# Attention, two expert layers and a planned order: five edits to the attention stage and its planner

## The chip, the cores and the metric

The kernel runs on one core of a Trainium2 chip, in one launch. The metric is device time in microseconds. Five engines have queues of their own that are worked off in order: TensorE (PE in the profile; PEld is its weight load, which runs beside its products), VectorE (DVE), ScalarE (ACT), GpSimd (POOL) and SyncE (SP, which here only issues DMAs). An engine waits for another through semaphores; whatever stands behind a waiting instruction in its queue waits too.

## The reference

Shapes: q, k, v are (4, 8, 1152, 64); the result of attention is taken as 2304 tokens of 512 values.

```python
q_pool = q.reshape(B, H, S // 2, 2, D).mean(axis=3)
scores = np.matmul(q_pool, k.transpose(0, 1, 3, 2)) / np.sqrt(D)
attn = np.exp(scores - np.max(scores, axis=-1, keepdims=True))
attn = attn / (np.sum(attn, axis=-1, keepdims=True) + 1e-09)
x = np.matmul(attn, v)                 # then (tokens, 512)
h = x @ w_in                           # 512 -> 2048
x = (h * np.cos(h)) @ w_out            # 2048 -> 512
expert = np.argmax(x @ w_gate, axis=1) # 8 experts, 512 -> 1024 -> 512
out[mask_e] = gate_w * (np.maximum(x[mask_e] @ w1[e], 0) @ w2[e])
```

## The kernel before, in words

The work has three stages: attention (lines 157 to 373), the first layer pair with the cosine (`layer1`, `layer2`, lines 802 to 836), and the experts (lines 862 to 880). The change touches attention, its planner, and the first weights of the second stage.

**Attention.** Two heads form a pair (the 64 values of a head fill half of the 128 rows), so there are 16 pairs, i = 0 to 15. For a pair, `load` (192) fetches q and K, `loadv` (200) V, `qadd` (204) adds the two halves of q that are pooled, `kh`, `qh` and `qt` (210 to 222) make rounded copies of K and Q on ScalarE. The maxima over keys are taken first, from products of the rounded copies: 14 tiles (t, g), of which t is a block of 128 queries (t = 4 the last half block) and g a third of the 1152 keys. `mx` (224) computes a tile into PSUM, `red` (236) reduces it on VectorE. `mneg` (250) joins the thirds and negates, `pmr` (256) turns the column into rows by a transposition on TensorE, `mrow` (261) copies them out of PSUM, and `mset` (266) brings them by DMA into row 0 and row 64 of the tile MR. The first pair does that in two parts, t = 0 to 2 and t = 3 and 4. The score step `s` (275) is a product of K and Q for one of 9 key blocks j and one of two halves hq of the queries, to which a product of a row of ones with MR adds the negated maximum. `exp` (283) is the exponential on ScalarE into a tile E, `es` (287) sums the E tiles on GpSimd, `pv` (294) multiplies with V into the accumulator o, and `ob`, `sum_`, `ln`, `rcp`, `nr1`, `nr2`, `norm` (300 to 332) divide by the sum and store the result in xT. The products of `s` and `mx` use TensorE as two row halves of 64, those of `pv` and `sum_` as two column halves: the row form and the column form.

**Splits.** Beside this, 32 jobs (`cload` to `cst`, lines 336 to 368) read the weights w_in and w_out, split each into a high and a low part on ScalarE and VectorE, and store them to the DRAM tensor ws. Each uses a PSUM bank of a pool `m` with a single buffer, which `pmr` and `sum_` use as well.

**The order** inside attention is written out by a planner. `steps` (33) lists every step with a due time, an engine, a cost in microseconds, what it reads and writes, and its pool. Due times are in units of their own: a pair takes 6 units, the s steps are a third of a unit apart, `pv` follows its s by 1.1 units, and split job n is due at 0.05 + 3 n. `plan` (102) then simulates: for each engine it looks among the pending steps that are due at most AHEAD units after the first pending one, and takes the one with the least

```python
late = max(0, t - free[e])*WAIT + P[n][0] + SWITCH*(e == "PE" and P[n][4] != mode)
```

that is, wait in us times WAIT, plus due time, plus SWITCH units if TensorE would have to change its form. The kernel's queues get the resulting order (371 to 373).

**The second stage** loads the 16 split weight tiles of 1 MB from ws (line 805) at its first block of 256 tokens, into tiles that share their memory with attention's, so that each load waits until what lay there is no longer read. `split_x` (638) prepares the first block of xT. For each weight tile, `layer1` (802) computes h by 12 products and passes it through nine steps on ScalarE and VectorE to g; `layer2` (829) multiplies g by the second half of the tile into po.

Of the kernel before, what the change touches and what calls it, by code (L numbers as in the profile page):

```python
# [28 lines left out]
AHEAD = {"PE": 5.4, "DVE": 3.6, "ACT": 3.0, "POOL": 3.9, "SP": 8.0}  # L29
WAIT, SWITCH = 2.75, 0.5  # L30


def steps(NP, NJ, J):


    P = []
# [5 lines left out]
    for i in range(NP):  # L42
        b = 6*i
        first = i == 0
        p = -101 if first else b - 11.8
        at(p - 9, "load", (i, 0), "SP", 0.6, (), [("qr", i)], ("qr", 2, ("qr", i)))
        at(p - 9, "load", (i, 1), "SP", 0.6, (), [("k", i)], ("k", 4, ("k", i)))
        at(b - 7, "loadv", (i,), "SP", 0.6, (), [("v", i)], ("v", 3, ("v", i)))
        at(p, "qadd", (i,), "DVE" if first else "POOL", 1.1 if first else 1.41, [("qr", i)], [("q", i)], ("q", 3, ("q", i)))
        at(p, "kh", (i, 0), "ACT", 0.63, [("k", i)], [("kh", i, 0)], ("kh", 2, ("kh", i, 0)))  # L50
        at(p + 0.5, "qh", (i,), "ACT", 0.63, [("q", i)], [("qh", i)], ("qh", 2, ("qh", i)))
        at(p + 1, "kh", (i, 1), "ACT", 0.63, [("k", i), ("kh", i, 0)], [("kh", i, 1)])
        at(-40 if first else p + 2.5, "qt", (i,), "ACT", 0.42, [("q", i)], [("qt", i % 2)])
        parts = ((0, 3), (3, 5)) if first else ((0, 5),)
        for lo, hi in parts:
            p = (-20 if lo else -100) if first else b - 8.95
            for n, (t, g) in enumerate(tiles):
                if lo <= t < hi:
                    x = p + n*(0.1 if first else 5.8/14)
                    ks = [[("kh", i, 0)], [("kh", i, 0), ("kh", i, 1)], [("kh", i, 1)]][g]  # L60
                    if t == 4: ks = [("kh", i, 0), ("kh", i, 1), ("qt", i % 2)]
                    else: ks = ks + [("qh", i)]
                    key = ("x", i, t, g)
                    at(x, "mx", (i, t, g), ROWS, 0.35 if (t, g) == (4, 0) else 0.18, ks, [key], ("s", 2, key) if first and n % 3 else ("x", 1, key))
                    at(x, "red", (i, t, g), "DVE", 0.56 if (t, g) == (4, 2) else 0.96, [key], [("mx", i, lo)])
            x = p + 2 if first else p + 5.7
            at(x, "mneg", (i, lo, hi), "DVE", 0.17, [("mx", i, lo)], [("mneg", i, lo)])
            at(x + 0.1, "pmr", (i, lo, hi), ROWS, 0.2, [("mneg", i, lo)], [("pmr", i, lo)], ("m", 1, ("pmr", i, lo)))
            at(x + 0.2, "mrow", (i, lo, hi), "DVE", 0.27, [("pmr", i, lo)], [("mrow", i, lo)])
            at(x + 0.2, "mset", (i, lo, hi), "SP", 2.4, [("mrow", i, lo)], [("mr", i, lo)])  # L70
        for hq in range(2):
            for j in range(J):
                m = b + 3*hq + j/3
                mr = [("mr", i, lo) for lo, hi in parts if hq or not lo]
                key = (i, hq, j)
                at(m, "s", key, ROWS, 0.617, [("k", i), ("q", i)] + mr, [("s", *key)], ("s", 2, ("s", *key)))
# [25 lines left out]
def plan(P):  # L102
# [15 lines left out]
    for i in range(1 + max(p[3][0] for p in P)):  # L118
        if ("kh", i, 1) in users:
            users["kh", i, 0] |= users["kh", i, 1]  # L120
# [818 lines left out]
```

## Time and profile before

| what | value |
|---|---|
| runs | 1249.96, 1252.36, 1255.13 us; median 1252.36 |
| profiled execution | 1250.38 us, its span 1248.7 us |
| granted TensorE clock, mean | 0.994 |
| TensorE busy | 1208.4 us, 97% of the span |
| VectorE, ScalarE, GpSimd busy | 872.7, 762.1, 432.9 us |
| attention | about 0 to 484 us |

A row of a timeline has the start and the length in us, the engine, the line of the kernel, the operation, what it writes and reads, how many instructions were merged, and in brackets the idle time of that engine before it and what ended it. SPq is SyncE's queue: a row there is the issue of a DMA, not its transfer. Products in fp32 appear as two instructions each, so one s step is four of line 279 and two of line 281, one pv step four of line 298.

### The profile page before, as it was taken

What the parts mean: (1) busy time and instruction counts of PE and PEld (TensorE: products, weight loads), DVE (VectorE), ACT (ScalarE), POOL (GpSimd) and SP (SyncE); (2) the same over time, 40 slices, a digit from 0 to 9 for tenths busy, and PEclk for the clock granted to TensorE, in tenths of its full rate; (3) what the DMA queues carried; (4) which work ended last, traced back from release to release, by engine and by line L of the source; (5) the groups of instructions that cost most, each with busy time, mean ns of one, the idle gap of its engine ahead of it and who ended that gap; (6) DMA issues with size and microseconds to landing.
All of it is one profiled execution on the core that took longest, in us unless ns stands there. A gap on an engine that the chain in (4) does not pass through costs nothing. (4 is left out here: it accounts for less than half of the span.)

```text
span 1248.7 us, 22742 instructions
## 1 busy us (share of the span) xinstructions
PE 1208.4 (97%) x8415; PEld 956.9 (77%) x8415; DVE 872.7 (70%) x1895; ACT 762.1 (61%) x1533; POOL 432.9 (35%) x380
## 2 busy tenths in 40 slices
PE   5999999999999998999999999999998999999997
PEld 2566666666665655899999999999987998999896
DVE  5877777777776743667767767777676877777761
ACT  2566666666666654565565565565574877677751
POOL 3678887888887784000000000000003121112100
PEclk9999999999999998999999999999999999999999
DMA  3644444444443348200000000000046997778720
GB/s 129 221 149 147 156 128 138 146 126 126 136 149 100 96 149 331 124 19 1 18 13 6 18 1 18 18 1 18 18 152 234 400 334 259 269 270 287 261 72 6
DMA packets 70411, 163.75 MB, mean 131 GB/s; under 512 B 7643, under 2 KB 24153, under 8 KB 68252
## 3 DMA queue, kind: packets, MB, share of 16 engines
q1 hardware_dynamic: 66300, 150.92, 35.1%
q0 software_dynamic: 4000, 11.38, 2.5%
q8 instruction: 66, 1.08, 0.4%
q14 instruction: 45, 0.37, 0.1%
HBM read 135.65 MB, written 28.39 MB: 131 GB/s over the span
## 5 line engine op out<-in xcount | busy, mean ns | idle before, releaser
L292 POOL TENSOR_TENSOR es<-es,E 128x576 f32<-128x576 f32 x192 | 277.6, 1446 | 33.8 <-ACT E L285 23.6
L285 ACT ACTIVATE E<-s 128x576 f32<-128x576 f32 x288 | 182.3, 652 | 111.2 <-PE s L281 104.4
L242 DVE TENSOR_REDUCE MX<-pmx 128x2 f32<-128x768 f32 x192 | 182.9, 957 | 88.8 <-PE pmx L231 88.0
L813 PE MATMUL h<-xh,wf 128*128 128x256 f32 x1152 | 233.1, 287 | 3.5 <-DMA wf<-ws 3.5
L834 PE MATMUL po<-wf,g 128*128 128x512 f32 x864 | 224.3, 395 | 4.3 <-ACT g L825 3.6
L813 PEld LDWEIGHTS h<-xh,wf 128*128 128x128 f32 x1152 | 189.9, 193 | 8.6 <-issue 4.2
L279 PE MATMUL s<-Q,K 64*128 64x288 f32 x1152 | 193.7, 420 | 1.9 <-ACT E L285 1.9
L679 POOL DMA_INDIRECT xg<-x2d,idx x25 | 27.5, 1099 | 474.1 <-ACT ar L818 390.3
L834 PEld LDWEIGHTS po<-wf,g 128*128 128x128 f32 x864 | 152.7, 189 | 33.4 <-ACT g L825 7.1
L668 DVE TENSOR_TENSOR w<-raw,w 128x1024 fp32r<-128x1024 f32 x128 | 154.3, 1221 | 22.0 <-ACT w L667 16.7
L298 PE MATMUL o<-E,vt 128*64 128x288 f32 x1152 | 165.5, 415 | 0.2 <-ACT E L285 0.2
L813 PE MATMUL h<-xl,wf 128*128 128x256 f32 x576 | 164.1, 285 | 0.0
L281 PE MATMUL s<-MR,ON 64*128 64x288 f32 x576 | 148.5, 511 | 0.0
L667 ACT CAST w<-raw 128x1024 fp32r<-128x1024 f32 x128 | 132.4, 1053 | 18.9 <-DMA raw<-in_moe_w_dram 10.3
L748 PE MATMUL po<-w,hh 128*128 128x512 f32 x600 | 142.6, 392 | 0.0
L748 PEld LDWEIGHTS po<-w,hh 128*128 128x128 f32 x600 | 110.9, 188 | 22.8 <-ACT hh L737 0.3
L822 ACT ACTIVATE ar<-ar 128x256 f32<-128x256 f32 x144 | 60.1, 417 | 98.9 <-DVE ar L821 98.5
L298 PEld LDWEIGHTS o<-E,vt 128*64 128x64 f32 x1152 | 73.6, 136 | 59.1 <-issue 19.4
L279 PEld LDWEIGHTS s<-Q,K 64*128 64x128 f32 x1152 | 96.8, 188 | 28.2 <-issue 14.6
L813 PEld LDWEIGHTS h<-xl,wf 128*128 128x128 f32 x576 | 111.1, 193 | 4.0
L713 PE MATMUL ph<-xh,w 128*128 128x256 f32 x576 | 111.4, 288 | 1.6 <-ACT xh L640 1.3
L824 DVE SCALAR_TENSOR_TENSOR ar<-ar,h 128x256 f32<-128x256 f32 x144 | 60.3, 419 | 54.1 <-ACT ar L823 54.0
(189 smaller groups left out, 1852.0 us busy)
## 6 DMA issues: line engine op xcount, KB each, us to landing
raw<-in_moe_w_dram SPq DMA_DIRECT2D x128, 512.0 KB
wf<-ws SPq DMA_DIRECT2D x16, 1024.0 KB
qr<-in_q_dram SPq DMA_DIRECT2D x16, 576.0 KB
K<-in_k_dram SPq DMA_DIRECT2D x16, 576.0 KB
vt<-in_v_dram SPq DMA_DIRECT2D x16, 576.0 KB
cv_t<-in_moe_w_in_dram SPq DMA_DIRECT2D x16, 512.0 KB
ws<-cv_o SPq DMA_DIRECT2D x32, 256.0 KB
cv_t<-in_moe_w_out_dram SPq DMA_DIRECT2D x16, 512.0 KB
```

The source lines that it names most:

```text
L242: nc.vector.reduce_max(out.rearrange("p (w g) -> p w g", g=3)[:, 2*t:2*t+2, g], p[:, :, :KG], axis=AX.X)
L279: nc.tensor.matmul(p[:, h, :NQ], lhsT=T["k", i][R[h], j*128:(j+1)*128], rhs=T["q", i][R[h], qs], start=True, stop=False)
L281: nc.tensor.matmul(p[:, h, :NQ], lhsT=ON[R[h]], rhs=MR[i % 3][R[h], qs], start=False, stop=True)
L285: nc.scalar.activation(e, T.pop(("s", i, hq, j))[:, :, :NQ], AF.Exp, scale=1.0/16)
L292: nc.gpsimd.tensor_add(T["es", i, hq], T["e", i, hq, 0] if j == 1 else T["es", i, hq], T["e", i, hq, j])
L298: nc.tensor.matmul(T["o", i, hq][64*h:64*h+64], lhsT=T["v", i][:, h, j], rhs=T["e", i, hq, j][:, h], start=(j == 0), stop=(j == J-1))
L667: nc.scalar.copy(w[:, 0], t)
L668: nc.vector.tensor_sub(w[:, 1], t, w[:, 0])
L713: nc.tensor.matmul(ph, lhsT=wt[k][:, a, m*128:(m+1)*128], rhs=x[k//2][y][:, k % 2], start=(c == 0), stop=(c == 3*KC-1))
L748: nc.tensor.matmul(po, lhsT=hs[m][:, y, q*128:(q+1)*128], rhs=wt[4 + m//2][:, a, (m % 2)*512:(m % 2)*512+512], start=(c == 0), stop=(c == ...
L813: nc.tensor.matmul(h, lhsT=w[:, a, k*128:(k+1)*128], rhs=x[k//2][y][:, k % 2], start=(n == 0), stop=(n == 3*KC-1))
L834: nc.tensor.matmul(pos[c][t], lhsT=g[:, y, t*128:(t+1)*128], rhs=W1[f][:, b, 512:], start=(f == 0 and i == 0), stop=(f == FT-1 and i == 2))
```

## The change

- The planner counts a change of form as 0.2 us into the column form and 0.1 into the row form, instead of 0.12 each; WAIT goes from 2.75 to 5.72, SWITCH from 0.5 to 0.7, and AHEAD changes for three engines. There are 12 E buffers instead of 10, and some costs and due times are altered.
- The loads of the first two pairs and the first V are due ahead of everything. The first pair's q and K are loaded, added and rounded in two pieces of columns each (the first 384, then the rest).
- The first part of the first pair's maxima goes to MR without a DMA: six products, each of one column of the maxima with the identity, write the rows to rows 0 and 64 of a PSUM bank, and VectorE and ScalarE copy one row each. The second part (t = 3 and 4) is due at -4 instead of -20.
- Split job n is due at 10.21 + 2.95 n, and from n = 27 on at 89 + 1.2 (n - 27).
- Four of the 16 weight tiles of the second stage get memory of their own, and are loaded from ws during attention, 8 units after the store that completes them is due.

```diff
...
 FETCH = {"load": 3.0, "loadv": 2.0, "cload": 2.0}
-AHEAD = {"PE": 5.4, "DVE": 3.6, "ACT": 3.0, "POOL": 3.9, "SP": 8.0}
-WAIT, SWITCH = 2.75, 0.5
+AHEAD = {"PE": 4.5, "DVE": 4.12, "ACT": 3, "POOL": 2.17, "SP": 8.0}
+CHANGE = {COLS: 0.2, ROWS: 0.1}
+EARLY = 4
+BEHIND = 1.1
+SPREAD = 5.1
+WAIT, SWITCH = 5.72, 0.7
...
-        p = -101 if first else b - 11.8
-        at(p - 9, "load", (i, 0), "SP", 0.6, (), [("qr", i)], ("qr", 2, ("qr", i)))
-        at(p - 9, "load", (i, 1), "SP", 0.6, (), [("k", i)], ("k", 4, ("k", i)))
-        at(b - 7, "loadv", (i,), "SP", 0.6, (), [("v", i)], ("v", 3, ("v", i)))
-        at(p, "qadd", (i,), "DVE" if first else "POOL", 1.1 if first else 1.41, [("qr", i)], [("q", i)], ("q", 3, ("q", i)))
-        at(p, "kh", (i, 0), "ACT", 0.63, [("k", i)], [("kh", i, 0)], ("kh", 2, ("kh", i, 0)))
-        at(p + 0.5, "qh", (i,), "ACT", 0.63, [("q", i)], [("qh", i)], ("qh", 2, ("qh", i)))
-        at(p + 1, "kh", (i, 1), "ACT", 0.63, [("k", i), ("kh", i, 0)], [("kh", i, 1)])
-        at(-40 if first else p + 2.5, "qt", (i,), "ACT", 0.42, [("q", i)], [("qt", i % 2)])
+        p = -101 if first else b - 12.5
+        early = -200 if i < 2 else b - 20.8
+        at(early, "load", (i, 0), "SP", 0.6, (), [("qr", i, 0)], ("qr", 2, ("qr", i, 0)))
+        at(early, "load", (i, 1), "SP", 0.6, (), [("k", i, 0)], ("k", 4, ("k", i, 0)))
+        if first:
+            at(early, "load", (i, 2), "SP", 0.6, [("k", i, 0)], [("k", i, 1)])
+            at(early, "load", (i, 3), "SP", 0.6, [("qr", i, 0)], [("qr", i, 1)])
+        at(-200 if first else b - 7, "loadv", (i,), "SP", 0.6, (), [("v", i)], ("v", 3, ("v", i)))
+        whole = range(1 + first)
+        for x in whole:
+            c = ((0.67, 0.33)[x] if first else 1)
+            at(p + 9*x, "qadd", (i, x), "DVE" if first and not x else "POOL", 1.45*c, [("qr", i, x)] + [("q", i, 0)]*x, [("q", i, x)], None if x else ("q", 3, ("q", i, 0)))
+            at(p + 0.1 + 9*x, "qh", (i, x), "ACT", 0.2 + 0.47*c, [("q", i, x)] + [("qh", i, 0)]*x, [("qh", i, x)], None if x else ("qh", 2, ("qh", i, 0)))
+        for x in range(2):
+            c = ((0.48, 0.76)[x] if first else 0.67)
+            at(p + (0.1 if first else 0.2 + 0.8*x), "kh", (i, x), "ACT", c, [("k", i, x*first)] + [("kh", i, 0)]*x, [("kh", i, x)], None if x else ("kh", 2, ("kh", i, 0)))
+        at(-4 if first else p + 2.5, "qt", (i,), "ACT", 0.48, [("q", i, whole[-1])], [("qt", i % 2)])
...
-            p = (-20 if lo else -100) if first else b - 8.95
+            p = (-4 if lo else -100) if first else b - 8.72
...
-                    x = p + n*(0.1 if first else 5.8/14)
+                    x = p + n*(0.1 if first else SPREAD/14)
...
-                    else: ks = ks + [("qh", i)]
+                    else: ks = ks + [("qh", i, x) for x in whole if t == 3 or not x]
...
-                    at(x, "mx", (i, t, g), ROWS, 0.35 if (t, g) == (4, 0) else 0.18, ks, [key], ("s", 2, key) if first and n % 3 else ("x", 1, key))
+                    at(x, "mx", (i, t, g), ROWS, 0.35 if (t, g) == (4, 0) else 0.19, ks, [key], ("s", 2, key) if p == -100 and n % 3 else ("x", 1, key))
...
-            x = p + 2 if first else p + 5.7
+            x = (-2 if lo else p + 2) if first else p + SPREAD
             at(x, "mneg", (i, lo, hi), "DVE", 0.17, [("mx", i, lo)], [("mneg", i, lo)])
+            if first and not lo:
+                at(x + 0.1, "pmq", (i,), ROWS, 1.2, [("mneg", i, lo)], [("pmr", i, lo)], ("m", 1, ("pmr", i, lo)))
+                for h in range(2):
+                    at(x + 0.2, "mput", (i, h), ("DVE", "ACT")[h], 0.45, [("pmr", i, lo)], [("mr", i, h - 2)])
+                continue
             at(x + 0.1, "pmr", (i, lo, hi), ROWS, 0.2, [("mneg", i, lo)], [("pmr", i, lo)], ("m", 1, ("pmr", i, lo)))
             at(x + 0.2, "mrow", (i, lo, hi), "DVE", 0.27, [("pmr", i, lo)], [("mrow", i, lo)])
             at(x + 0.2, "mset", (i, lo, hi), "SP", 2.4, [("mrow", i, lo)], [("mr", i, lo)])
...
                 m = b + 3*hq + j/3
-                mr = [("mr", i, lo) for lo, hi in parts if hq or not lo]
+                mr = [("mr", i, x) for x in ([-2, -1] + [3]*hq if first else [0])]
...
-                at(m, "s", key, ROWS, 0.617, [("k", i), ("q", i)] + mr, [("s", *key)], ("s", 2, ("s", *key)))
-                at(m, "exp", key, "ACT", 0.65, [("s", *key)], [("e", *key)], ("e", 10, ("e", *key)))
+                at(m, "s", key, ROWS, 0.617, [("k", i, x) for x in whole] + [("q", i, x) for x in whole if x < 1 or hq] + mr, [("s", *key)], ("s", 2, ("s", *key)))
+                at(m, "exp", key, "ACT", 0.65, [("s", *key)], [("e", *key)], ("e", 12, ("e", *key)))
...
-                    at(m, "es", key, "POOL", 1.41, [("e", *key)] + [("e", i, hq, 0)]*(j == 1), [("es", i, hq)], ("es", 2, ("es", i, hq)) if j == 1 else None)
-                at(m + 1.1, "pv", key, COLS, 0.486, [("v", i), ("e", *key)], [("o", i, hq)], ("o", 1, ("o", i, hq)) if j == 0 else None)
-            m = b + 3*hq + 4
+                    at(m, "es", key, "POOL", 1.45, [("e", *key)] + [("e", i, hq, 0)]*(j == 1), [("es", i, hq)], ("es", 2, ("es", i, hq)) if j == 1 else None)
+                at(m + BEHIND, "pv", key, COLS, 0.486, [("v", i), ("e", *key)], [("o", i, hq)], ("o", 1, ("o", i, hq)) if j == 0 else None)
+            m = b + 3*hq + max(3.84, BEHIND + 2.7)
...
-            at(m + 0.3, "nr2", key, "DVE", 0.6, [("r0", *key)], [("nr", *key)])
+            at(m + 0.3, "nr2", key, "DVE", 0.46, [("r0", *key)], [("nr", *key)])
...
-        x = 0.05 + 3*n
+        x = 10.21 + 2.95*n if n < 27 else 89 + 1.2*(n - 27)
...
         at(x + 0.1, "cst", (n,), "SP", 1.2, [("co", n)], [("ws", n)])
+        f = n - 4*(n//8) - 4
+        if n % 8 > 3 and f < EARLY:
+            at(x + 8, "wload", (f,), "SP", 0.6, [("ws", m) for m in range(n + 1)], [("w", f)])
...
-    for i in range(1 + max(p[3][0] for p in P)):
-        if ("kh", i, 1) in users:
-            users["kh", i, 0] |= users["kh", i, 1]
+    for k in users:
+        if k[0] in ("kh", "qh", "k", "q", "qr") and k[2]:
+            users[k[0], k[1], 0] |= users[k]
...
-        end[n] = free[e] = t + p[5] + 0.12*(e == "PE" and p[4] != mode)
+        end[n] = free[e] = t + p[5] + (CHANGE[p[4]] if e == "PE" and p[4] != mode else 0)
...
-        raw, kp, vp, ep, sm, cv = pool("a_raw", 2), pool("a_k", 4), pool("a_v", 3), pool("a_e", 10), pool("a_sm", 2), pool("a_cv", 2)
+        raw, kp, vp, ep, sm, cv = pool("a_raw", 2), pool("a_k", 4), pool("a_v", 3), pool("a_e", 12), pool("a_sm", 2), pool("a_cv", 2)
...
+        def part(i, x, n, of):
+
+            return slice(n*x, of if x or i else n)
+
         def load(i, x):
-            if x:
-                T["k", i] = kp.tile([128, S], F32, tag="k", name="K")
-                nc.sync.dma_start(T["k", i], k[i])
+            if x in (0, 3):
+                if x == 0:
+                    T["qr", i] = raw.tile([128, 2, SQ], F32, tag="qr", name="qr")
+                cs = part(i, x // 3, KG, SQ)
+                nc.sync.dma_start(T["qr", i][:, :, cs], q[i].rearrange("p (t n) -> p t n", t=2)[:, :, cs])
             else:
-                T["qr", i] = raw.tile([128, 2, SQ], F32, tag="qr", name="qr")
-                nc.sync.dma_start(T["qr", i], q[i].rearrange("p (t n) -> p t n", t=2))
+                if x == 1:
+                    T["k", i] = kp.tile([128, S], F32, tag="k", name="K")
+                cs = part(i, x - 1, KG, S)
+                nc.sync.dma_start(T["k", i][:, cs], k[i][:, cs])
...
-        def qadd(i):
-
-            T["q", i] = kp.tile([128, SQ], F32, tag="q", name="Q", bufs=3)
-            qr = T.pop(("qr", i))
-            (nc.gpsimd if i else nc.vector).tensor_add(T["q", i], qr[:, 0], qr[:, 1])
+        def qadd(i, x):
+
+            if x == 0:
+                T["q", i] = kp.tile([128, SQ], F32, tag="q", name="Q", bufs=3)
+            cs = part(i, x, KG, SQ)
+            qr = T["qr", i]
+            (nc.gpsimd if i or x else nc.vector).tensor_add(T["q", i][:, cs], qr[:, 0, cs], qr[:, 1, cs])
...
         def kh(i, x):
             if x == 0:
                 T["kh", i] = kp.tile([128, S], F32R, tag="kh", name="KH", bufs=2)
-            cs = slice(x*SQ, (x+1)*SQ)
+            cs = slice(x*SQ, (x+1)*SQ) if i else part(i, x, KG, S)
             nc.scalar.copy(T["kh", i][:, cs], T["k", i][:, cs])
 
-        def qh(i):
-            T["qh", i] = kp.tile([128, SQ], F32R, tag="qh", name="QH", bufs=2)
-            nc.scalar.copy(T["qh", i], T["q", i])
+        def qh(i, x):
+            if x == 0:
+                T["qh", i] = kp.tile([128, SQ], F32R, tag="qh", name="QH", bufs=2)
+            cs = part(i, x, KG, SQ)
+            nc.scalar.copy(T["qh", i][:, cs], T["q", i][:, cs])
...
-            here, tag = (ps_s, "s") if i == 0 and tiles.index((t, g)) % 3 else (ps_x, "x")
+            here, tag = (ps_s, "s") if i == 0 and t < 3 and g else (ps_x, "x")
...
+        def pmq(i):
+
+            T["pmr", i, 0] = p = small("pmq")
+            for h in range(2):
+                for t in range(3):
+                    nc.tensor.matmul(p[64*h:64*h+1, t*128:(t+1)*128], lhsT=T["mneg", i, 0][:, 2*t+h:2*t+h+1], rhs=ident, start=True, stop=True)
+
+        def mput(i, h):
+            (nc.scalar.copy if h else nc.vector.tensor_copy)(MR[i % 3][64*h:64*h+1, :384], T["pmr", i, 0][64*h:64*h+1, :384])
...
+        def wload(f):
+            nc.sync.dma_start(W1[f].bitcast(F32), ws[f])
...
-        wp = [pool(f"w{j}", 1) for j in range(FT)]
+        wp = wp + [pool(f"w{j}", 1) for j in range(len(wp), FT)]
...
-        W1 = []
...
         def layer1(c, f):
-            if c == 0:
+            if c == 0 and f >= EARLY:
                 W1.append(wp[f].tile([128, 2, 1024], F32R, tag="w", name="wf"))
                 nc.sync.dma_start(W1[f].bitcast(F32), ws[f])
...
+        wp = [ctx.enter_context(tc.tile_pool(name=f"w{j}", bufs=1)) for j in range(EARLY)]
+        W1 = [p.tile([128, 2, 1024], F32R, tag="w", name="wf") for p in wp]
+        attention(nc, tc, q, k, v, xT, ident, w_in, w_out, ws, x2d, W1)
+        moe(nc, tc, magic, rp, xT, ws, w_gate, x2d, w1, w2, out, ident, W1, wp)
...
```

## Rows read from the trace of the kernel before

**Rows 1.** Windows: busy us by engine, PEclk, DMA share, GB/s; mid-attention.

```profile
228.06:256.12 28.06, 28.06 (x226) 17.56 (x224) 20.94 (x31) 18.39 (x34) 23.36 (x20) 1.00 0.43 139
```

**Rows 2.** Timeline of TensorE, mid-attention, two equal places of the cycle.

```profile
201.66 1.68 PE L298 MATMUL o<-E,vt 128*64 128x288 f32 x12
...
229.71 1.68 PE L298 MATMUL o<-E,vt 128*64 128x288 f32 x12
```

**Rows 3.** Timeline, all engines, end of attention.

```profile
467.88 1.19 PE L298 MATMUL o<-E,vt 128*64 128x288 f32 x8
...
469.00 0.76 PE L279 MATMUL s<-Q,K 64*128 64x288 f32 x4
...
470.43 0.71 PE L298 MATMUL o<-E,vt 128*64 128x288 f32 x4
...
471.06 0.76 PE L279 MATMUL s<-Q,K 64*128 64x288 f32 x4
...
480.18 0.76 PE L279 MATMUL s<-Q,K 64*128 64x288 f32 x4
...
480.99 0.71 PE L298 MATMUL o<-E,vt 128*64 128x288 f32 x4
```

**Rows 4.** Timeline, all engines, start.

```profile
4.81 0.76 DVE L208 TENSOR_TENSOR Q<-qr 128x576 f32<-128x576 f32 x1 [3.74 <-DMA qr<-in_q_dram]
...
6.23 0.67 ACT L214 CAST KH<-K 128x576 fp32r<-128x576 f32 x1 [4.12 <-DMA K<-in_k_dram]
...
7.52 1.58 PE L231 MATMUL pmx<-KH,QH 64*128 64x384 f32 x6 [7.52 <-ACT QH L218]
...
8.25 7.87 DVE L242 TENSOR_REDUCE MX<-pmx 128x2 f32<-128x768 f32 x9 [2.68 <-PE pmx L231]
...
16.48 0.37 PE L259 MATMUL pmr<-ident,mneg 128*6 128x128 f32 x1 [2.21 <-DVE mneg L254]
...
19.37 0.42 SPq L195 DMA_DIRECT2D K<-in_k_dram  x1
...
22.09 1.33 PE L279 MATMUL s<-Q,K 64*128 64x288 f32 x4
...
23.45 1.17 PE L279 MATMUL s<-Q,K 64*128 64x288 f32 x4
...
24.54 1.24 ACT L214 CAST KH<-K 128x576 fp32r<-128x576 f32 x2 [16.09 <-DMA K<-in_k_dram]
...
26.78 1.19 ACT L285 ACTIVATE E<-s 128x576 f32<-128x576 f32 x2
```

**Rows 5.** Waits of TensorE, 22.09 to 60 us: total, times, longest.

```profile
PE pmx L231 <- DVE MX L242: 3.9, 4, 2.0
...
PE pmx L231 <- ACT QH L218: 1.6, 1, 1.6
```

**Rows 6.** Timeline, all engines, hand-over to the second stage.

```profile
473.03 17.68 SPq L805 DMA_DIRECT2D wf<-ws  x13
...
483.80 0.66 PE L308 MATMUL psum<-E,ones 128*64 128x288 f32 x4
...
486.43 0.35 PE L813 MATMUL h<-xh,wf 128*128 128x256 f32 x1 [1.98 <-DMA wf<-ws]
...
490.51 0.55 PE L813 MATMUL h<-xh,wf 128*128 128x256 f32 x1 [1.50 <-DMA wf<-ws]
...
495.53 2.42 PE L834 MATMUL po<-wf,g 128*128 128x512 f32 x8 [0.53 <-ACT g L825]
```

**Rows 7.** Windows: columns as rows 1; 2 us after hand-over and later.

```profile
490.00:492.00 2.00, 1.49 (x7) 1.52 (x8) 0.73 (x2) 1.24 (x2) 0.00 (x0) 0.50 1.03 434
498.00:500.00 2.00, 2.00 (x16) 1.86 (x15) 0.59 (x3) 1.36 (x4) 0.00 (x0) 1.00 1.05 442
```

**Rows 8.** Page, costliest groups: busy, mean ns | idle before, releaser.

```profile
L824 DVE SCALAR_TENSOR_TENSOR ar<-ar,h 128x256 f32<-128x256 f32 x144 | 60.3, 419 | 54.1 <-ACT ar L823 54.0
```

**Rows 9.** Timeline of SyncE's queue, the second pair's row DMAs.

```profile
52.10 0.69 SPq L271 DMA_DIRECT2D MR<-mrow  x1
```

More of the change, by code (lines that the diff above doesn't have):

```diff
@@ L87, in steps @@
             at(m + 0.3, "nr1", key, "DVE", 0.46, [("sum", *key), ("r0", *key)], [("nr", *key)], ("nr", 2, ("nr", *key)))
-            at(m + 0.3, "nr2", key, "DVE", 0.6, [("r0", *key)], [("nr", *key)])
+            at(m + 0.3, "nr2", key, "DVE", 0.46, [("r0", *key)], [("nr", *key)])
             at(m + 0.4, "norm", key, "POOL", 0.95, [("nr", *key), ("ob", *key)], [("xT", *key)])
     for n in range(NJ):
-        x = 0.05 + 3*n
+        x = 10.21 + 2.95*n if n < 27 else 89 + 1.2*(n - 27)
         at(x - 5, "cload", (n,), "SP", 0.6, (), [("ct", n)], ("ct", 2, ("ct", n)))
-        at(x, "cabs", (n,), "ACT", 0.64, [("ct", n)], [("ca", n)], ("m", 1, ("ca", n)))
+        at(x, "cabs", (n,), "ACT", 0.65, [("ct", n)], [("ca", n)], ("m", 1, ("ca", n)))
         for c in range(1, 5):
@@ L154, in plan, with attention @@
     return [P[n][2:4] for _, n in sorted(out)]
-def attention(nc, tc, q, k, v, xT, ident, w_in, w_out, ws, x2d):
+def attention(nc, tc, q, k, v, xT, ident, w_in, w_out, ws, x2d, W1):
     NP, _, S = k.shape
@@ L597, in finish, with moe @@
         return sel
-def moe(nc, tc, magic, rp, xT, ws, w_gate, x2d, w1, w2, out, ident):
+def moe(nc, tc, magic, rp, xT, ws, w_gate, x2d, w1, w2, out, ident, W1, wp):
     FT = ws.shape[0]
@@ L896, in body @@
         xT = [rp.tile([128, 1024], F32, tag="raw", name="xT").rearrange("p (k n) -> p k n", n=CH) for c in range(NT // CH)]
-        attention(nc, tc, q, k, v, xT, ident, w_in, w_out, ws, x2d)
-        moe(nc, tc, magic, rp, xT, ws, w_gate, x2d, w1, w2, out, ident)
+        wp = [ctx.enter_context(tc.tile_pool(name=f"w{j}", bufs=1)) for j in range(EARLY)]
+        W1 = [p.tile([128, 2, 1024], F32R, tag="w", name="wf") for p in wp]
+        attention(nc, tc, q, k, v, xT, ident, w_in, w_out, ws, x2d, W1)
+        moe(nc, tc, magic, rp, xT, ws, w_gate, x2d, w1, w2, out, ident, W1, wp)
 _INS = ["q", "k", "v", "moe_w_in", "moe_w_out", "moe2_w_gate", "moe2_w1", "moe2_w2"]
```

## The prediction

> **What bounds the kernel now.** The span is 1248.7 us, of which attention takes the first 484. I read the busy time by stretches first. A stretch of 28 us in mid-attention [rows 1] shows TensorE busy throughout, while POOL, the next busiest engine, is at 23.36 of 28.06 us, VectorE at 20.94 and ScalarE at 18.39. Attention is therefore bound by TensorE, except where that engine stands still.
>
> The timeline of TensorE was read next. The same place in the cycle, a run of three o steps, comes back after 229.71 - 201.66 = 28.05 us [rows 2], so one pair of heads costs 28.05 us. In between TensorE enters the column form (o, psum) six times, counting one of the two runs that rows 2 show. What such a trip costs comes from the end of the stage [rows 3]. Two s steps and the change after them take 470.43 - 469.00 = 1.43 us, one takes 480.99 - 480.18 = 0.81: a further s costs 0.62 and the change into the column form 0.19. Two o steps and the change back take 469.00 - 467.88 = 1.12, one takes 471.06 - 470.43 = 0.63: a further o costs 0.49, the change back 0.14. A round trip costs 0.33 us. Over a pair, six trips are 2.0 us of the 28.05, and nothing but these can shrink there.
>
> Two places are not dense. At the **start** [rows 4] the first product waits until 7.52 us for QH. The nine reductions that follow are VectorE's (8.25 to 16.12), the first s stands at 22.09 and the first exponential at 26.78, behind the KH cast of the next pair. That cast waited, with ScalarE idle for 16.09 us, for a K load issued only at 19.37 us, because SyncE's queue had the maxima's DMA ahead of it. From the first s on TensorE waits another 3.9 + 1.6 us for maxima and QH [rows 5]. Its first s takes 23.45 - 22.09 = 1.36 us against 0.62 later, which is the lower of its two clock levels (1.2 against 2.4 GHz), although the granted clock of the page shows no fall there. At the **hand-over** [rows 6, 7] the last psum starts at 483.80, but the first h waits 1.98 us for its weights, the second 1.50 us, and the clock falls: 0.50 granted in 490 to 492 us, where seven matmuls take 1.49 us (0.21 each) against 16 in 2.00 us (0.125) at 498. The waiting began in SyncE's queue, where 13 of the 16 weight loads were issued between 473.03 and 490.71.
>
> **The change, part by part.**
>
> *Loads in pieces, next pair's loads moved up.* The two loads of 576 KB show their receivers starting 1.42 us apart (4.81 and 6.23) [rows 4], so about 405 KB per us move once the queue runs. The first q piece (384 KB) needs 0.47 us less than the whole: about 4.3 us. K's first third (192 KB) lands 0.47 us later, 4.8; the rest of K at 5.7, the rest of q at 6.2. The q sum (two thirds of the work that now lasts from 4.81 to 5.57) ends by 4.9, the smaller KH and QH casts follow at 4.85 and 5.3, and the first product starts near 5.8 instead of 7.52: **-1.7 us**. SyncE issues three more loads ahead (v and the next pair's two, some 0.46 us each, as between its neighbours); they go behind the first four pieces and delay none. The next pair's K then lands near 11 us, since 2.9 MB at that rate are 7 us after the first latency of 4, and ScalarE's 16 us wait ends.
>
> The trace of before has no smaller load, so the rate of a piece is bounded by that of the whole and half of it; I take the whole's, since pieces in one queue run into one another as the two loads did. The Trainium skill says the opposite ("DMA: Bandwidth & Descriptors", Bandwidth: transfers should be batched to 1 MiB or more to keep three quarters of the peak, with 138 GB/s at 64 KB and 341 at 1 MB). By an estimate from that page the two first pieces would lose about 1 us together, and the forecast would be 1238; the trace's two loads can't decide it.
>
> *First row of maxima by small products.* Removed ahead of the first s: the transposition, the row copy and two DMAs of that part. Also, the three remaining tiles of t=3 and two of t=4, with their reductions and a second transposition, stood between 16.78 and 22.09; the due time of -4 now lets them run among the s steps. Added: six products of one column by 128, two copies of 384 elements. A transposition of 128 moving columns (at 16.48) lasts 0.37 us at the low clock [rows 4]; six in a row are 2.2 us, overlapping halves of the array would give about half, 1.1. I take 2.0, nearer the row. A copy of 576 elements on ScalarE costs 1.24/2 = 0.62 us [rows 4], so 384 cost 0.45, both copies at once on two engines. With the last of nine reductions at 16.12 - 1.7 = 14.4 us, the negated maxima at 14.7, the products end at 16.9 and the s steps can start there: **-5.2 us** (16.9 against 22.09), the first exponential near 18.6 instead of 26.78. Between that and 60 us TensorE lost 5.5 us by waits [rows 5] and about 4 x 0.74 = 3.0 us by the low clock in its first four s. After the change the waits for ScalarE are gone, but the leftover maxima compete through their one PSUM buffer, and the clock must still rise; I leave 6.0 of the 8.5: **-2.5 us**. The start gives -7.7 (bounds -2, if the leftover maxima stall as the whole phase did, and -10).
>
> *Splits later, 12 E buffers.* The weight splits start 10 planner units (some 47 us) later, and the last five come closer together (1.2 units, some 5.6 us apart) in the last 35 us. VectorE and ScalarE have 7 and 9.6 us free per 28 us [rows 1] and in the last pair no maxima are left, so the cover is there: nothing. If it is not, a bank shared by splits and sums keeps the last psum waiting, up to one split of some 5 us.
>
> *Four weight tiles fetched in attention.* Four loads of 1 MB move from the hand-over into a stage whose DMA share is 0.43 [rows 1]; SyncE issues each in half a us, due 8 units after the store that it reads. They hide. At the hand-over the first h can follow the last psum at 484.5 instead of 486.43, the second needs no load, and without those waits the clock should stay up. Three h at 12 x 0.125 = 1.5 us run to 489.0, and the first po then waits only for its g, the chain that ends at 495.53 now. That chain lost time behind the second h's late arrival; without it, its nine operations of some 0.42 us [rows 8] with a table load beside them bring po near 490: -5.5 us. VectorE, with five of them (2 us) per h against TensorE's 1.5, will give some back while the pipeline fills; I take **-4.5** (bounds -2, the two waits less a new one of that size, and -6).
>
> *Planner's weights.* It now prices a change as 0.2 and 0.1 us, close to the rows' 0.19 and 0.14. It stays in a form until the other is 0.7 units ahead (0.5 before). With o due 1.1 units behind s and three s to a unit, the old band is 3 steps wide, 18/3 = 6 trips, as seen; the new one gives 4.2 steps, 4.3 trips. Against it, waiting is priced at 5.72 a us, not 2.75. The third s of a run waits about 0.18 us for its PSUM buffer (one exponential of 0.65 and two hand-shakes against one s and one maximum), which now costs 1.0 units, more than the 0.7 of a change; it cost 0.5, no more than one. Where that decides, runs break after two s: 9 trips. A maximum ahead of the run takes most of the wait away. Ends: 4.3 trips, -1.7 x 0.33 x 15 = -8.4 us; 9 trips, +14.9 us. I take 5.5, nearest to the six that the trace shows: **-2.5 us**.
>
> **Sum.** -7.7 - 4.5 - 2.5 = -14.7 us. The profiled execution took 1250.38 us (span 1248.7), 2.0 below the median of 1252.36: it gives 1235.7, and with half of that distance 1237.
>
> **Rivals.**
> - *Fewer trips still*, 4.3 per pair: about 1231 us. For it: the wider band, 12 E buffers. Against: the s steps need fillers, and there are 15 for 18.
> - *Runs of two*, 9 trips in mid-attention: 1250.4 - 12.2 + 14.9 = 1253 us, no change. For it: rows 3 show two and two where no maxima are left.
> - *Runs of one or two, slower*: the same mechanism beyond 10 trips a pair. One trip more per pair costs 15 x 0.33 = 5 us, so the 12.2 us of the two ends are eaten at 8.5 trips and the result is 0.5% slower from 9.8 on; at 12 trips 1250.4 - 12.2 + 29.7 = 1268 us. Rows 3 show one s followed by o at 480.18, where it was the end of the work.
> - *The start gives only its lower bound*, since the leftover maxima hold the s steps: 1243 us.
>
> **How the numbers follow.** Forecast (5 to 7 trips, both ends gained) 0.60; fewer trips 0.16; start at its lower bound 0.08; runs of two 0.09; slower 0.07. About 0.5% (6.3 us) is what a measurement of this kernel can tell from no change. Faster by more holds the first three, a little less for the edge of the last of these: 0.82; within it 0.11; slower 0.07. The range takes the forecast's bounds (start +5.7, hand-over +2.5 at the worst, not both with a bad order) and most of the first rival: 1227 to 1248.
>
> **What would show it.** First product near 5.8 us, first exponential near 18.6, the second pair's row DMAs (now at 52.10 [rows 9]) near 44; no wait of h for wf, and the granted clock at 1.00 through the hand-over; the period of a pair at 27.5 to 28.0. A period above 28.4 with more than seven trips, or s steps waiting for maxima after 17 us, makes it wrong.

## The result, and the profile after

The changed kernel takes 1235.66 us in the median of four runs (1234.87 to 1237.27), against 1252.69 for the kernel before (four runs): a ratio of 0.9866, 95% interval 0.9843 to 0.9889, so 17 us or 1.3% faster. The forecast was 1237. Its profiled execution has a span of 1233.9 us, 14.7 less than before. The landmarks show where these went (times in us, each from the timeline of TensorE; "16th h" is the end of the last product of the 16th h step, and "the rest" runs from there to the end of the span):

| | before | after | difference |
|---|---|---|---|
| psum of the fourth pair, first half | 136.56 | 132.25 | -4.3 |
| psum of the thirteenth pair, first half | 389.05 | 386.06 | -3.0 |
| end of the last psum (attention) | 484.46 | 480.69 | -3.8 |
| first h after that end | +1.97 | -0.07 | -2.0 |
| 16th h after the start of the first h | 46.64 | 39.19 | -7.5 |
| the rest | 715.6 | 714.1 | -1.5 |

So attention gave only 3.8 us and the hand-over 9.5. The rest lies between 714.1 and 716.9 in all the profiles of this case, so its -1.5 can't be told from that scatter.

**Start.** The timeline of all engines, first 24 us of the kernel after:

```profile
4.24 0.56 DVE L238 TENSOR_TENSOR Q<-qr 128x384 f32<-128x384 f32 x1 [3.17 <-DMA qr<-in_q_dram]
...
4.76 0.51 ACT L244 CAST KH<-K 128x384 fp32r<-128x384 f32 x1 [2.65 <-DMA K<-in_k_dram]
...
5.73 0.69 PE L263 MATMUL pmx<-KH,QH 64*128 64x384 f32 x2 [5.73 <-ACT QH L250]
...
6.89 0.83 ACT L244 CAST KH<-K 128x768 fp32r<-128x768 f32 x1 [1.21 <-DMA K<-in_k_dram]
7.48 0.59 POOL L238 TENSOR_TENSOR Q<-qr 128x192 f32<-128x192 f32 x1 [3.14 <-DMA qr<-in_q_dram]
...
8.50 7.01 DVE L274 TENSOR_REDUCE MX<-pmx 128x2 f32<-128x768 f32 x8 [1.08 <-PE pmx L263]
...
15.86 1.82 PE L312 MATMUL pmq<-ident,mneg 128*1 128x128 f32 x12 [2.21 <-DVE mneg L286]
...
17.80 0.55 DVE L315 CAST MR<-pmq 1x384 fp32r<-1x384 f32 x1 [2.08 <-PE pmq L312]
18.38 0.47 ACT L315 CAST MR<-pmq 1x384 fp32r<-1x384 f32 x1 [10.66 <-DVE MR L315]
18.87 0.93 ACT L250 CAST QH<-Q 128x192 fp32r<-128x192 f32 x2
...
19.71 1.24 ACT L244 CAST KH<-K 128x576 fp32r<-128x576 f32 x2
19.77 1.16 PE L321 MATMUL s<-Q,K 64*128 64x288 f32 x4
...
20.85 1.03 ACT L254 CAST QT<-Q 64x64 fp32r<-64x64 f32 x4
...
21.90 0.65 ACT L327 ACTIVATE E<-s 128x576 f32<-128x576 f32 x1
```

The first product comes at 5.73 us, as forecast (5.8). But the second KH cast waits until 6.89, the ninth reduction ends at 8.50 + 7.01 = 15.51 instead of 14.4, and the row of maxima is followed by two copies that run one behind the other: ScalarE's waits for VectorE's. That wait stands at the head of ScalarE's queue, which is idle for 10.66 us before 18.38 while the casts of QH, of the next pair's KH and of QT (18.87 to 21.88) stand behind it, and ahead of the first exponential at 21.90. The forecast had 18.6.

**Mid-attention.** The timeline of TensorE, the same place in two successive cycles of the kernel after:

```profile
201.75 0.71 PE L340 MATMUL o<-E,vt 128*64 128x288 f32 x4
...
229.95 0.71 PE L340 MATMUL o<-E,vt 128*64 128x288 f32 x4
```

A pair costs 28.20 us instead of 28.05 [rows 2], with seven trips into the column form instead of six (125 in all of attention instead of 105). Over the nine pairs between the two psum landmarks that is 1.35 us lost, and the table shows 1.3.

**Hand-over.** The timeline of TensorE, kernel after, and then the windows (columns as in rows 1):

```profile
480.03 0.66 PE L350 MATMUL psum<-E,ones 128*64 128x288 f32 x4
480.62 0.39 PE L857 MATMUL h<-xh,wf 128*128 128x256 f32 x1
...
487.13 0.39 PE L857 MATMUL h<-xh,wf 128*128 128x256 f32 x1 [0.49 <-DVE ar L868]
...
488.66 1.55 PE L878 MATMUL po<-wf,g 128*128 128x512 f32 x6
```

```profile
480.50:490.50 10.00, 9.51 (x72) 8.93 (x71) 7.57 (x21) 7.04 (x16) 2.08 (x3) 1.00 1.01 421
490.50:500.50 10.00, 10.00 (x67) 9.15 (x66) 7.62 (x22) 6.78 (x19) 0.32 (x2) 1.00 1.02 424
```

The first h follows the psum without a wait [rows 6: it waited 1.98 us], the granted clock stays at 1.00 [rows 7: 0.50], and the first po comes at 488.66 instead of 495.53, after five h instead of three. In the two stretches of 10 us TensorE is busy 9.51 and 10.00 us and does 72 and 67 products. Its waits from the last psum to the end of the 16th h (total, times, longest), in the kernel before and then after:

```profile
PE h L813 <- DMA wf<-ws: 3.5, 2, 2.0
PE po L834 <- ACT g L825: 2.3, 6, 0.5
...
PE h L857 <- DVE ar L868: 0.5, 1, 0.5
```

From the first h to the end of the 16th, both kernels do the same 192 products of h and 67 of po. Before, 1.5 us of that stretch are the second h's wait for weights, 2.3 the waits of po for its g, and 2.2 the low clock of the first two h (2.58 and 2.90 us against 1.70 and 1.60 after). Less the one wait of 0.5 us after, that is 5.5 of the 7.5 us; the other 2.0 stand under no wait of the trace.

Both sources put five h ahead of the first po (`LAG = 4`). TensorE works its queue off in order, and the trace has three h there in before, e1 and e12, and five in every kernel that fetches tiles early. So the number is an order that was fixed when the kernel was built, and not an effect of the run; why the built order differs, no run shows.

### The profile page after: what moved, and what is told of

Its sections match the earlier page's. It is cut to its first block, busy times and chain, and to the rows that moved or that the text cites. A ratio compares the mean times of both kernels' runs of the same rounds, so it can differ in the third digit from the quotient of the medians.

```text
span 1233.9 us, 22751 instructions
## 1 busy us (share of the span) xinstructions
PE 1205.3 (98%) x8426; PEld 952.8 (77%) x8426; DVE 873.1 (71%) x1895; ACT 761.3 (62%) x1535; POOL 430.8 (35%) x381
## 5 line engine op out<-in xcount | busy, mean ns | idle before, releaser
L334 POOL TENSOR_TENSOR es<-es,E 128x576 f32<-128x576 f32 x192 | 274.0, 1427 | 35.3 <-ACT E L327 25.3
L340 PE MATMUL o<-E,vt 128*64 128x288 f32 x1152 | 169.1, 417 | 0.2 <-ACT E L327 0.2
```

The lines of the kernel that those rows point to most:

```text
L334: nc.gpsimd.tensor_add(T["es", i, hq], T["e", i, hq, 0] if j == 1 else T["es", i, hq], T["e", i, hq, j])
L340: nc.tensor.matmul(T["o", i, hq][64*h:64*h+64], lhsT=T["v", i][:, h, j], rhs=T["e", i, hq, j][:, h], start=(j == 0), stop=(j == J-1))
```

## The experiments

The landmarks of each kernel's profile, with the median of its runs (a trip is an entry of TensorE into the column form):

| kernel | median us | trips | us per pair | attention ends | first h waits for weights | first h to end of 16th |
|---|---|---|---|---|---|---|
| before | 1252.69 | 105 | 28.05 | 484.46 | 1.98 | 46.64 |
| after | 1235.66 | 125 | 28.20 | 480.69 | 0 | 39.19 |
| e1, after, no prefetch | 1250.62 | 125 | 28.20 | 480.64 | 9.96 | 43.62 |
| e2, before + prefetch | 1240.15 | 105 | 28.06 | 483.58 | 0 | 39.22 |
| e3, after, row by DMA | 1234.33 | 119 | 28.20 | 477.75 | 0 | 39.18 |
| e4, after, whole loads | 1236.31 | 125 | 28.20 | 481.46 | 0 | 39.18 |
| e5, after, five trips | 1241.84 | 83 | 27.97 | 484.81 | 0 | 40.58 |
| e6, after, splits early | 1252.69 | 141 | 28.64 | 493.53 | 0 | 40.44 |
| e7, after, casts first | 1234.99 | 124 | 28.20 | 477.43 | 0 | 39.18 |
| e8, e5 and e7 | 1242.10 | 83 | 27.97 | 485.47 | 0 | 40.57 |
| e9, e3 and e7 | 1233.83 | 119 | 28.20 | 477.61 | 0 | 39.19 |
| e10, e2 + early loads | 1235.67 | 107 | 28.06 | 479.51 | 0 | 39.21 |
| e11, e10 + casts, late second part | 1235.66 | 110 | 28.06 | 480.17 | 0 | 39.22 |
| e12, before + early loads | 1245.47 | 107 | 28.06 | 479.54 | 4.20 | 45.11 |

**The prefetch, taken out and put in alone.** Edit of e1, against the kernel after:

```diff
-EARLY = 4
+EARLY = 0
```

> The changed kernel with EARLY = 0: no weight tile is fetched in attention, all else as changed. Theory: the hand-over is worth about 9 us (2 us before the first h, 7 us while the first 16 h run, because five h instead of three stand ahead of the first po and none waits for weights), so about 1244.5 us, with the 16th h again some 46 us after the first instead of 39. Rival: the prefetch is worth only the waits that the trace of before shows for weights (2.0 + 1.5 us) and the rest comes from the new order of attention: about 1239 us.

Measured 1250.62 us, no different from the kernel before (ratio 1.0003, 0.9990 to 1.0016): both expectations were too small. Attention ends where it did, but the first h waits 9.96 us and the 16 h take 4.4 us longer, 14.4 in all. The timeline of TensorE in e1, that of SyncE's queue (with the last line from the kernel before), and what that queue waited for from 425 to 500 us (total, times, longest), in e1 and then in the kernel before:

```profile
479.98 0.66 PE L350 MATMUL psum<-E,ones 128*64 128x288 f32 x4
490.59 0.55 PE L857 MATMUL h<-xh,wf 128*128 128x256 f32 x1 [9.96 <-DMA wf<-ws]
```

```profile
476.18 0.52 SPq L410 DMA_DIRECT2D ws<-cv_o  x1
483.07 15.19 SPq L849 DMA_DIRECT2D wf<-ws  x13
...
469.93 0.58 SPq L368 DMA_DIRECT2D ws<-cv_o  x1
```

```profile
SPq L849 <- DMA ws<-cv_o: 18.6, 4, 6.3
...
SPq L805 <- DMA ws<-cv_o: 7.7, 3, 2.8
```

The last store of a split is issued at 476.18, and the bulk of the weight loads, 13 of 16, only from 483.07 on; in four waits the loads stood 18.6 us for stores. Before, the last store came at 469.93, that bulk from 473.03 on [rows 6], and the loads stood 7.7 us. So in the changed order the stores come late, the weight loads behind them too, and the prefetch pays for that. That the splits' due times make them late, and not the other weights of the planner, is likely and not isolated: no run has the new weights with the old due times of the splits and no prefetch. Edit of e2, against the kernel before (`moe` as in the change):

```diff
+        f = n - 4*(n//8) - 4
+        if n % 8 > 3 and f < EARLY:
+            at(x + 8, "wload", (f,), "SP", 0.6, [("ws", m) for m in range(n + 1)], [("w", f)])
...
-            if c == 0:
+            if c == 0 and f >= EARLY:
```

> The kernel before with the four weight tiles fetched in attention and nothing else: planner, due times and start as before. Theory: about 9 us faster than before, 1243.5 us, with the first h right behind the last psum and the 16th h some 39 us after the first. Rival (only the shown waits): 3.5 to 4 us faster, about 1249 us.

Measured 1240.15 us, ratio 0.9920 (0.9904 to 0.9937): 11 us, against the 9 of the theory and the 4 of the rival. The timeline of TensorE in e2:

```profile
482.92 0.66 PE L312 MATMUL psum<-E,ones 128*64 128x288 f32 x4
483.50 0.39 PE L819 MATMUL h<-xh,wf 128*128 128x256 f32 x1
```

The first h stands right behind the psum, the granted clock stays at 1.00, and 16 h take 39.22 us instead of 46.64, the same 7.4 us as in the change. This edit alone is worth two thirds of the result.

**Early loads, with and without it.** Edit of e12, against the kernel before; e10 is e2 with the same edit:

```diff
-        at(p - 9, "load", (i, 0), ...
-        at(p - 9, "load", (i, 1), ...
-        at(b - 7, "loadv", (i,), ...
+        early = -200 if i < 2 else p - 9
+        at(early, "load", (i, 0), ...
+        at(early, "load", (i, 1), ...
+        at(-200 if first else b - 7, "loadv", (i,), ...
```

> The kernel before with the weight tiles fetched in attention, and with the loads of the first two pairs and the first V due ahead of everything; planner, splits, row of maxima and single-piece loads as before. Theory: the start's gain of the change is the early loads (ScalarE no longer waits 16 us for the second K): attention ends some 4 us before the 483.58 of the prefetch alone, at about 479.5, with 28.05 us a pair, and the time is about 1236 us. Rival: the pieces and small products carried it: attention ends at 482 to 483, 1239.5 us.

Measured 1235.67 us (ratio 0.9889, 0.9862 to 0.9916), attention ends at 479.51: the theory held in both numbers. Prefetch and early loads alone, with the planner's weights, splits, pieces and small products left as before, give the time of the whole change (0.9866, 0.9843 to 0.9889) as far as the intervals can tell.

> The kernel before with the loads of the first two pairs and the first V due ahead of everything, and nothing else; the weight tiles are fetched at the hand-over as before. Theory: the weight loads wait for attention's tiles, so they move up with its end: attention ends near 480.4 (4.1 us earlier, as between the prefetch with and without early loads), the first h again waits about 2 us, and the time is about 4 us less than that of before. Rival: the weight loads are bound by the splits' stores or by their own rate, the first h waits longer, and nothing is gained, as where the changed kernel lost its prefetch.

Measured 1245.47 us, ratio 0.9957 (0.9938 to 0.9976): 5 to 6 us, by the interval 3 to 8. The theory held for the stage (479.54) and missed at the hand-over, as the timeline of TensorE in e12 shows:

```profile
478.88 0.66 PE L309 MATMUL psum<-E,ones 128*64 128x288 f32 x4
483.73 0.55 PE L814 MATMUL h<-xh,wf 128*128 128x256 f32 x1 [4.20 <-DMA wf<-ws]
```

The first h waits 4.20 us instead of 1.98; about 2 us of the gain are taken back there, though 16 h ran 1.5 us shorter.

**The first row of maxima and the loads in pieces.** Edit of e3, against the kernel after (the step then runs through `pmr`, `mrow` and `mset`, as the second part does):

```diff
-            if first and not lo:
-                at(x + 0.1, "pmq", ...
-                for h in range(2):
-                    at(x + 0.2, "mput", ...
-                continue
...
```

> The changed kernel with the first row of maxima brought as before: transposition, copy and two DMAs in place of six products and two copies. The forecast put 5.2 us on this edit and on the leftover maxima together. Theory: only the route differs, some 4.5 us (0.4 + 0.3 + two issues of 0.6 + about 2 to land) against 3.2 us measured for the products and the copies, so the first s ends about 1.3 us later and the time is about 1237 us. Rival: the DMA is the whole delay, +4 us or more, about 1240 us.

Measured 1234.33 us (1232.11 to 1235.93): not slower, and attention ends 2.9 us earlier. Both expectations failed. The timeline of all engines in e3:

```profile
11.89 1.24 ACT L239 CAST KH<-K 128x576 fp32r<-128x576 f32 x2 [3.34 <-DMA K<-in_k_dram]
...
15.56 0.37 PE L286 MATMUL pmr<-ident,mneg 128*6 128x128 f32 x1 [2.20 <-DVE mneg L281]
...
22.11 1.33 PE L316 MATMUL s<-Q,K 64*128 64x288 f32 x4
...
23.74 0.65 ACT L322 ACTIVATE E<-s 128x576 f32<-128x576 f32 x1 [9.64 <-PE s L318]
```

The first s starts at 22.11 instead of 19.77, yet nothing stands in front of the first exponential: ScalarE has been idle for 9.64 us before it, since without a copy in its queue the next pair's casts had run from 11.89 on. The 2.3 us that the products win on the way are lost behind that copy. The copy need not be all of e3's gain: its order also has six trips fewer than the change, all ahead of the fourth pair's first psum. Edit of e4, against the kernel after:

```diff
-                cs = part(i, x // 3, KG, SQ)
+                cs = slice(0, SQ)
...
-                cs = part(i, x - 1, KG, S)
+                cs = slice(0, S)
```

(with the loads of the second pieces left out)

> The changed kernel with the first pair's q and K each loaded in one piece (the casts and sums stay in pieces). Theory: the first product comes at about 6.6 to 7 us instead of 5.73, but the 1.1 us for which the reductions waited for the second piece of K go, so the ninth reduction ends at most 0.5 us later and the time stays within 0.7 us of 1235.7. Rival (the forecast's -1.7 us is real and kept to the end): 1237.4 us.

Measured 1236.31 us (1235.70 to 1238.91), 0.65 over the change, as expected; the runs of the two overlap. The timeline of all engines in e4:

```profile
4.74 0.56 DVE L235 TENSOR_TENSOR Q<-qr 128x384 f32<-128x384 f32 x1 [3.67 <-DMA qr<-in_q_dram]
...
6.22 0.51 ACT L241 CAST KH<-K 128x384 fp32r<-128x384 f32 x1 [4.11 <-DMA K<-in_k_dram]
...
7.93 7.87 DVE L271 TENSOR_REDUCE MX<-pmx 128x2 f32<-128x768 f32 x9 [2.63 <-PE pmx L260]
```

The nine reductions end at 7.93 + 7.87 = 15.80, 0.3 us later than with pieces. With two whole loads the last receiver starts at 6.22 us, with four pieces at 7.48. In the change 768 KB took from 4.24 to 7.48 us, 237 KB per us, where the second whole load of e4 took 1.48 us for 576 KB, 389 KB per us; in both, loads of V and of the next pair follow in the queue. Those did not take the difference, as the windows of 4 to 6 us show for all that the core's DMA engines moved (columns as in rows 1; the change, then e4):

```profile
4.00:6.00 2.00, 0.27 (x2) 0.27 (x2) 0.56 (x1) 0.92 (x2) 0.34 (x1) 1.00 0.95 266
...
4.00:6.00 2.00, 0.00 (x0) 0.00 (x0) 0.56 (x1) 0.00 (x0) 1.28 (x2) 1.00 1.03 410
```

With the pieces the DMA engines, at a busy share of 0.95, moved 266 GB/s; with whole loads, at 1.03, they moved 410. The Trainium skill ("DMA: Bandwidth & Descriptors", Bandwidth) advises transfers of 1 MiB or more for three quarters of the peak. The trace agrees in part: the smaller pieces were slower, but the 576 KB load, below that size as well, moved at 389 KB per us.

**ScalarE's queue at the start.** Edit of e7, against the kernel after:

```diff
-        p = -101 if first else b - 12.5
+        p = -101 if first else -100.5 if i == 1 else b - 12.5
...
-            at(p + 9*x, "qadd", ...
-            at(p + 0.1 + 9*x, "qh", ...
+            at(p + 1.4*x, "qadd", ...
+            at(p + 0.1 + 1.5*x, "qh", ...
...
-        at(-4 if first else p + 2.5, "qt", ...
+        at(-98.4 if first else p + 2.5, "qt", ...
```

> The changed kernel with ScalarE's casts of the rest of Q and of the second pair's K and Q due ahead of the row copies, in the 10.7 us in which it stood idle. Theory: the first s starts at about 18 us instead of 19.77 and the first exponential at about 20 instead of 21.90, and some of it is kept: 1234 us. Rival: the leftover maxima set the pace until 40 us, nothing is kept: 1235.7 us.

Measured 1234.99 us (1233.62 to 1235.53). The timeline of all engines in e7:

```profile
11.41 1.24 ACT L244 CAST KH<-K 128x576 fp32r<-128x576 f32 x2 [2.84 <-DMA K<-in_k_dram]
...
17.80 1.16 PE L321 MATMUL s<-Q,K 64*128 64x288 f32 x4
...
18.08 0.47 ACT L315 CAST MR<-pmq 1x384 fp32r<-1x384 f32 x1 [4.45 <-DVE MR L315]
...
19.27 0.65 ACT L327 ACTIVATE E<-s 128x576 f32<-128x576 f32 x1 [0.73 <-PE s L323]
```

The casts now run from 6.59 to 13.6 us, the first s starts at 17.80, the first exponential at 19.27, and attention ends 3.3 us earlier, more than expected. All of that stands at the first psum already (41.61 us against 44.93) and is kept to the end of attention. The median is lower by 0.7 us only; the rest after the 16th h was 716.9 us in this profile and 714.1 in that of the change, so that the stage's gain stands in the trace and is not settled by the times. e9 joins both edits:

> The changed kernel with the first row of maxima by DMA and with ScalarE's casts ahead of it. The row by DMA alone ended attention at 477.75 us instead of 480.69, the casts first alone at 477.43. Theory: both take the same lost time away (ScalarE's casts standing between the row and the exponentials, TensorE waiting for QH), so together they do little more than either: attention ends at 476 to 478, 1234 us. Rival: they add, 474.5 us, and 1231.5 us.

Attention ends at 477.61, so the theory held: both remove the same wait. With 1233.83 us (1232.27 to 1234.91) e9 has the lowest median here, 1.8 us under the change's, but the two were not timed side by side and their runs meet at the edge (the change's begin at 1234.87); that it beats the change is likely, not shown. e11 adds to e10 what e7 and the change do at the start (second pair's `p` at -100.5, `qt` at -98.4, second part of the maxima at -4):

> The last one with, in addition, the second pair's casts due early and the second part of the first maxima due at -4 instead of -20, as in the change. Six trips and 28.05 us a pair stay. Theory: the first s no longer stands behind the leftover maxima and the start gains another 3 to 4 us: attention ends at about 476, 1232.5 us, better than the changed kernel without its planner weights, late splits, pieces and small products. Rival: the leftover maxima only move and nothing is gained: 1236 us.

Measured 1235.66 us: the rival. The fourth pair's psum comes 0.9 us earlier than in e10, and the last pairs lose 1.5 again.

**Trips.** Edit of e5, against the kernel after:

```diff
-WAIT, SWITCH = 5.72, 0.7
+WAIT, SWITCH = 2.75, 1.0
```

> The changed kernel with WAIT 2.75 and SWITCH 1.0 instead of 5.72 and 0.7: the planner's order then has 5 changes into the column form per pair in mid-attention instead of 7 (83 in all against 125). Theory: a trip costs 0.33 us by the rows, but six trips took 28.05 us and seven 28.20, so more than half of a saved trip comes back as waits: about 27.9 us a pair, 4 us less in all, 1231.5 us. Rival: the waits for exponentials eat all of it (longer runs of s need fillers that aren't there): 28.2 us a pair or more, 1236 to 1240 us. Second rival: the full 0.33 a trip: 27.5 us a pair, about 1225 us.

Measured 1241.84 us, ratio to before 0.9920 (0.9906 to 0.9933): 6 us slower than the change. The period does fall, to 27.97 us, but the first psum comes 4.5 us later (49.44 against 44.93), and the last three and a half pairs take 98.3 us instead of 94.6. In that last stretch TensorE waits 5.8 us in all instead of 2.1, which is the difference. Most of it is for exponentials (total, times, longest; e5, then the change):

```profile
PE s L321 <- ACT E L327: 3.3, 6, 1.8
PE pmx L263 <- DVE MX L274: 1.3, 2, 1.1
...
PE s L321 <- ACT E L327: 1.5, 1, 1.5
```

Why the first psum comes later, e5 doesn't show. e8 has the same order with the casts first:

> Both of the last: five trips a pair and the casts first. Theory: the gains add, about 1230 us. Rival: no better than either alone.

Measured 1242.10 us, and attention ends at 485.47: nothing adds. Edit of e6, against the kernel after:

```diff
-        x = 10.21 + 2.95*n if n < 27 else 89 + 1.2*(n - 27)
+        x = 0.05 + 3*n
```

> The changed kernel with the splits due as before (0.05 + 3 n). The planner's order then has 9 trips per pair in mid-attention instead of 7 (141 in all). Theory: two trips more at 0.15 to 0.33 us each give 28.5 to 28.9 us a pair, and the splits again compete in the first 60 us: 1241 to 1248 us. Rival: the place of the splits changes nothing but which gaps they fill: 1236 us.

Measured 1252.69 us, the time of the kernel before: more than expected. The timeline of TensorE in e6, the same place in two cycles:

```profile
202.68 0.71 PE L350 MATMUL psum<-es,ones 128*64 128x288 f32 x4
...
231.32 0.71 PE L350 MATMUL psum<-es,ones 128*64 128x288 f32 x4
```

A pair costs 28.64 us, as the theory had it, and attention ends 12.8 us later than in the change. With the new weights the planner needs the late splits; with the old weights (e10) it makes 28.06 us a pair without them.

## Why the prediction was right, and where it was not

The time, 1235.66, is close to the 1237 of the forecast, but by terms that cancel: the start gave 3.4 us less than forecast, the planner cost 1.3 instead of giving 2.5, and the hand-over gave 5.0 more. That the sum came out is luck.

- **Start, forecast -7.7 us: -4.3**, inside its bounds. In the kernel before, the early loads alone give 4.1 (e10 against e2). The first product was right to 0.1 us. The step that failed is taking the whole load's rate for a piece: the pieces moved 237 KB per us and not 405, K's rest was cast at 6.89 and not near 5.7, and the reductions ended 1.1 us late. The second is the pair of copies: priced at 0.45 us side by side, they ran one behind the other, and the one in ScalarE's queue kept the casts behind it waiting; e7, which moves those casts and the sum of Q's rest ahead, ends attention 3.3 us earlier. The sum has a slip there too: 14.7 us and products of 2.0 end at 16.7, and the copy's 0.45 behind them stands nowhere. Small products were credited with part of 5.2 us; e3 shows them to be worth nothing as placed.
- **Second pair's row DMAs near 44 us**: they were issued at 52.42 [rows 9: 52.10]. As a landmark it was badly chosen, since by 60 us TensorE had done 22 s steps instead of 18.
- **Planner, forecast -2.5 us: +0.15 us a pair**, 1.3 us lost over the nine pairs between the landmarks. There were seven trips, not 5.5. Which of the two opposite effects that the prediction named won is not isolated, since the number hangs on the splits' due times as well: nine trips with the old ones (e6), five with the other two weights of e5. The price of a trip was wrong too. Periods of 27.97, 28.05, 28.20 and 28.64 us at 5, 6, 7 and 9 trips are 0.08 to 0.22 us a trip, not 0.33. Why a trip costs less over a cycle than the gaps beside it is open: TensorE has no idle time in these cycles, so no wait is shown that shorter runs could save. e5 shows that fewer trips can even cost 6 us. As the slower rivals went by the same price, they were priced too high.
- **Hand-over, forecast -4.5 us: -9.5**, beyond the lower bound of -6. The mechanism was right, and e2 shows it alone: no wait for weights, no fall of the clock. The step that failed is the end of the sum at the first po, put 5.5 us closer to the psum behind three h, with 1 us given back after it. It came only 3.1 us closer (7.97 us after the psum instead of 11.07), because five h run ahead of it, and 6.4 more were gained behind it: two h of 1.4 us each no longer stand there, and the 2.3 us for which po waited for its g are gone. The prediction took the order of h and po from the trace of before, and the change altered that order.
- **Splits later, costed at nothing**: they are not. e6, which undoes them, takes 17 us more, with nine trips a pair. At the hand-over, the profiles show the prefetch to be worth 14.4 us in the changed kernel (e1) and 9.5 in the kernel before (e2). The prediction looked for cover in VectorE's and ScalarE's free time; that the stores come late, and the weight loads that wait for them, it did not name.

What stays open: how much of the start's 4.3 us each of early loads, pieces and due times carries in the changed kernel, and whether e9 or e7 beats it by more than the scatter of the last two stages.

## What to carry to other kernels

At a change of stage, count the work that can run ahead of the first dependent step, not only the waits: 3.5 us of shown waits for weights were worth 9 to 11 us, since a low clock (2.2 us), later waits for g (2.3) and an order with three h instead of five came with them. A wait at the head of an in-order queue costs what stands behind it, so a copy that shortens its own path by 2 us can give it all back. And a planner's price for a change of form should be fitted to the period of whole cycles (here 0.08 to 0.22 us), not to the gap beside one change (0.33).

## What was not expected of the hardware

At the start TensorE's clock rose and fell again, and the granted clock shows only a part of it. The timeline of TensorE in the kernel after, and the window of 27 to 29 us (columns as in rows 1):

```profile
24.02 0.65 PE L321 MATMUL s<-Q,K 64*128 64x288 f32 x4
...
25.24 0.62 PE L266 MATMUL pmx<-KH,QT 128*128 128x384 f32 x2 [0.44 <-DVE MX L274]
25.79 1.11 PE L321 MATMUL s<-Q,K 64*128 64x288 f32 x4
...
27.40 1.16 PE L321 MATMUL s<-Q,K 64*128 64x288 f32 x4
```

```profile
27.00:29.00 2.00, 2.00 (x11) 1.34 (x9) 0.96 (x1) 0.81 (x2) 1.84 (x3) 0.50 0.00 0
```

The first s, at 19.77, takes 1.16 us (1.2 GHz), the one at 24.02 takes 0.65 (2.4 GHz), and those at 25.79 and 27.40 again 1.11 and 1.16. Ahead of this fall the engine had stood idle 1.06 us before 23.74, 0.44 before 25.24, and for most of 13.66 to 19.28. The granted clock reads 0.50 from 27 to 29 us, so the fall is recorded. It reads 1.00 up to 25 us, though the s at 19.77 ran at the lower level: the trace's first record of the clock stands at 22.65 us (32.85 in the kernel before). Ahead of that the level is read from the durations.
